# Two cached-attention problems on one core: wo loaded last in runs of up to 16 KB, with every head placed by selector matmuls

## The chip, the cores and the metric

The kernel runs on one core of one Trainium2 chip. The metric is the time of one execution on the device, in microseconds. A program on one core has only this one core's span to report. The profile's span starts at the first instruction and is about 1.7 us shorter than the timed execution (831.1 against 832.8 us in the profiled run of the kernel before).

## The reference

Two independent attention problems, A and B, with one query token each, 32 heads of 128 dimensions, and their results side by side:

```python
q      = (x @ wq) -> 32 heads x 128                 # x: 512, wq: 512 x 4096
k, v   = cache[:, Sk-W:, :]                         # A: W = 16384 keys, B: W = 4096 keys
p      = softmax(q . k / sqrt(128))
o      = p . v                                      # 32 x 128
out    = o.reshape(4096) @ wo                       # wo: 4096 x 512 (4 MB in bf16)
result = concat(out_A, out_B)                       # 1024 numbers
```

A head of A needs 4 MB of keys and 4 MB of values, and so do four heads of B together. With wq and wo of both problems the core must read 352 MB. The arithmetic on them is small.

## The kernel before

The work comes in units of 4 MB of keys: one head of A, or four heads of B. Each group of four heads of A is followed by one unit of B. A unit has two chunks of 64 keys per partition. For each chunk VectorE multiplies keys by the query (`prod`) and adds the halves (`half`), PE sums the rest into PSUM (`red`) with identity matmuls, VectorE and ACT make the exponentials, and PE multiplies them with the values into `acc` (PV). Loads all go through one queue, issued by SP in program order as buffers come free:

```python
def _load_kv(nc, cx, unit, which, k=0, w=2 * U):
    ...
    for g, h in enumerate(unit.heads):
        src = view[h].rearrange("(p l) d -> p l d", p=P // n)       # 32 KB in a row per partition
        cx.o(nc.sync.dma_start(out=t[g:P:n, k : k + w, :], in_=src[:, k : k + w, :]))
```

After four heads a group ends: PE folds `acc` to 4 rows of 128 (`f_ps`), ACT divides by the sums (`orow`), and 16 tiny matmuls turn the 4 rows into a column form, 128 partitions by 4, whose row order fits a piece of wo with 4 KB in a row per partition:

```python
def _fin_col(nc, cx, gr):
    gr.oc_ps = cx.pst_pool.tile([P, G], F32, tag="ocp", name="oc_ps")
    orow_j = gr.orow[:, :].rearrange("o (a j) -> o j a", j=G)
    for j in range(G):
        for g in range(G):
            cx.o(nc.tensor.matmul(
                gr.oc_ps[32 * g : 32 * g + 32, j : j + 1],
                lhsT=orow_j[:, j, :], rhs=cx.ident[0:G, g : g + 1], start=True, stop=True,
            ))
```

So wo is loaded in pieces of 1 MB between the units' keys and values (`[g p (j f)]`, 4 KB runs), each group adds its 4 output matmuls, and only the last group must be quick. That last group has a path of its own: the last head of A comes last of all, its V is loaded in pieces of 64, 32, 16 and 16 keys, the last 512 KB of wo (in 1 KB runs) stand ahead of the last two pieces, and the last 32 keys' values are used as matmul weights, so that their result is a column at once:

```python
    load_v(u, 0, U)
    load_v(u, U, U - LATE)
    load_wo(stA, last_wo, 1)
    load_v(u, 2 * U - LATE, LATE // 2)
    load_v(u, 2 * U - LATE // 2, LATE // 2)
...
def _late_pv(nc, cx, ch, gr):
    for k in range(U - LATE, U):
        cx.o(nc.tensor.matmul(
            gr.f_ps[:, 0, :], lhsT=u.vt[:, ch.k0 + k, :], rhs=ch.p[:, k // 4, :, k % 4],
            start=False, stop=(k == U - 1), skip_group_check=True,
        ))
def _late_out(nc, cx, gr):
    ... # multiply by 1/sum on VectorE, 8 output matmuls, 2 copies, output DMA
```

The softmax here doesn't subtract the row's maximum and nothing guards it: scores larger than these inputs give would overflow.

## Time and profile before

| | kernel before |
|---|---|
| timed, median (3 runs) | 832.32 us |
| span of the profile | 831.1 us |
| read from HBM | 352.32 MB |
| busy: DMA engines / VectorE / PE / ACT | nearly all of the span / 70% / 50% / 8% |
| last packet of V ends (packet records of the trace) | 826.1 us |

From the page of the kernel before: the span, the share of each engine, the DMA rows of the 40 slices (busy tenths of the 16 DMA engines, and GB/s), and the DMA queues. Queue q1 carries the kernel's loads, q8 instructions that are fetched through the same engines.

```profile
span 831.1 us, 6096 instructions
PE 416.9 (50%) x2512; PEld 142.0 (17%) x2512; DVE 585.1 (70%) x299; ACT 68.6 (8%) x301; POOL 2.9 (0%) x16
...
DMA  9999999999999999999999999999999999999996
GB/s 379 429 436 428 423 442 431 431 428 431 431 430 428 429 429 428 429 432 434 428 431 432 431 427 429 427 432 433 429 430 432 433 431 427 431 429 428 427 427 256
DMA packets 16047, 352.71 MB, mean 424 GB/s; under 512 B 2578, under 2 KB 3092, under 8 KB 5268
...
q1 hardware_dynamic: 15732, 352.33, 99.1%
q8 instruction: 19, 0.31, 0.2%
```

The DMA engines are busy in every slice but the last, at about 430 GB/s. No other engine comes near. So there is almost no gap in the stream of loads, and with the bytes fixed only the time per byte, the first microseconds and the last ones are left to work on.

The table of stretches shows the end. Its columns are the stretch, its length, busy time (and instructions) of PE, PEld, DVE, ACT and POOL, the granted PE clock, the DMA share and GB/s.

```profile
700.00:780.00 80.00, 40.33 (x252) 13.61 (x251) 57.40 (x28) 7.32 (x33) 0.00 (x0) 0.70 1.00 429
...
820.00:821.00 1.00, 1.00 (x24) 0.29 (x12) 0.00 (x0) 0.00 (x0) 0.00 (x0) 1.00 0.98 369
821.00:822.00 1.00, 1.00 (x12) 0.48 (x8) 0.00 (x0) 0.59 (x1) 0.00 (x0) 1.00 0.75 265
823.00:824.00 1.00, 1.00 (x19) 0.47 (x10) 0.15 (x1) 0.36 (x1) 0.00 (x0) 1.00 0.56 211
825.00:826.00 1.00, 1.00 (x7) 0.43 (x5) 0.00 (x0) 0.79 (x2) 0.00 (x0) 1.00 0.15 61
```

The 16 DMA engines do not finish together: the share falls from about 1 at 821 us to nothing at 826 us. PE is busy for the whole of every microsecond from 816 to 827 us.

The last values' packets ended at 826.1 us, and from the end of a load's last packet to an instruction that waits for it about 0.5 us passes.

### The profile page before, as it was taken

How to read it: one execution, taken by the hardware profiler on the slowest of the kernel's cores; microseconds unless marked ns; L12 is line 12 of the kernel's file. 1: busy time of each engine (PE TensorE's matmuls, PEld its weight loads, DVE VectorE, ACT ScalarE, POOL GpSimd, SP SyncE). 2: the span in 40 equal slices, each digit the busy share in tenths (PEclk: the TensorE clock that was granted, in tenths of full speed). 3: DMA queues.
4: the chain of work that ended last, by engine and by line, in shares of the span. 5: the costliest groups of instructions: out<-in, count | busy, mean ns of one | idle time of the engine just before them, and what ended most of it. 6: DMA issues, size and time to landing. Idle time of an engine off the chain costs nothing.

```text
span 831.1 us, 6096 instructions
## 1 busy us (share of the span) xinstructions
PE 416.9 (50%) x2512; PEld 142.0 (17%) x2512; DVE 585.1 (70%) x299; ACT 68.6 (8%) x301; POOL 2.9 (0%) x16
## 2 busy tenths in 40 slices
PE   3357444544454445544455543555554534555356
PEld 1112111211121111211112111121111211121113
DVE  1893667777777766777777776677667776677793
ACT  2100001000110001100010000100001000110011
POOL 1000000000000000000000000000000000000000
PEclk9768657776777656777678657686667767667658
DMA  9999999999999999999999999999999999999996
GB/s 379 429 436 428 423 442 431 431 428 431 431 430 428 429 429 428 429 432 434 428 431 432 431 427 429 427 432 433 429 430 432 433 431 427 431 429 428 427 427 256
DMA packets 16047, 352.71 MB, mean 424 GB/s; under 512 B 2578, under 2 KB 3092, under 8 KB 5268
## 3 DMA queue, kind: packets, MB, share of 16 engines
q1 hardware_dynamic: 15732, 352.33, 99.1%
q8 instruction: 19, 0.31, 0.2%
q14 instruction: 8, 0.07, 0.0%
q10 hardware_dynamic: 288, 0.00, 0.0%
HBM read 352.32 MB, written 0.00 MB: 424 GB/s over the span
## 4 chain that ended last, share of the span: by engine, by line
DMA 65%; DVE 22%; issue 10%; PE 2%; SPq 1%; DVEq 0%; ACTq 0%
DMA kt<-in_A_k_cache_dram 53%; DVE prod L177 13%; DMA kt<-in_B_k_cache_dram 9%; DVE half L189 7%; DMA xTB<-in_B_x_dram 3%; DVE sc L219 2%; SPq L170 1%; PE acc L248 0%; PE red L202 0%; DVE xbB L96 0%; PE late_ps L278 0%; PE outB L386 0%; PE late_ps L290 0%; PE f_ps L345 0%; PE out L324 0%
## 5 line engine op out<-in xcount | busy, mean ns | idle before, releaser
L202 PE MATMUL red<-half,ident 128*128 128x512 bf16 x640 | 258.1, 576 | 380.3 <-DVE half L189 380.3
L177 DVE TENSOR_TENSOR prod<-kt,qallA 128x8192 bf16<-128x8192 bf16 x64 | 283.2, 4426 | 160.1 <-DMA kt<-in_A_k_cache_dram 159.3
L189 DVE TENSOR_TENSOR half<-prod 128x4096 bf16<-128x4096 bf16 x80 | 182.5, 2281 | 0.0
L202 PEld LDWEIGHTS <-ident 128*128 128x128 bf16 x640 | 82.6, 129 | 530.0 <-issue 505.4
L177 DVE TENSOR_TENSOR prod<-kt,qallB 128x8192 bf16<-128x8192 bf16 x16 | 70.8, 4426 | 50.8 <-DMA kt<-in_B_k_cache_dram 50.5
L248 PE MATMUL acc<-vt,pA 128*16 128x512 bf16 x1016 | 88.0, 478 | 11.9 <-DMA vt<-in_A_v_cache_dram 11.9
L226 ACT ACTIVATE pA<-sc 128x64 bf16<-128x64 f32 x64 | 16.4, 256 | 518.2 <-DVE sc L219 518.2
L219 DVE TENSOR_REDUCE sc<-red 128x64 f32<-128x512 f32 x80 | 54.7, 684 | 3.7 <-PE red L202 3.7
L248 PEld LDWEIGHTS <-pA 128*16 128x16 bf16 x1016 | 23.3, 99 | 81.3 <-issue 74.7
L226 ACT ACTIVATE p_sb<-sc,off 128x64 bf16<-128x64 f32 x64 | 21.5, 336 | 104.4 <-DVE sc L219 104.4
L248 PE MATMUL acc<-vt,p_sb 128*16 128x512 bf16 x256 | 23.6, 512 | 0.0
L345 PE MATMUL f_ps<-acc_sb,sel 128*4 128x128 f32 x120 | 15.5, 272 | 4.7 <-ACT acc_sb L259 4.7
L259 ACT COPY acc_sb<-acc 128x512 f32<-128x512 f32 x16 | 9.4, 586 | 83.0 <-PE acc L248 83.0
L124 PE MATMUL q_ps<-wq_t,xbA 128*128 128x512 bf16 x32 | 9.1, 455 | 13.7 <-DVE xbA L96 13.7
L226 ACT ACTIVATION_READ_ACCUMULATOR p_sb<-sc,off 128x1 f32 x64 | 11.9, 186 | 0.0
L226 ACT ACTIVATION_READ_ACCUMULATOR pA<-sc 128x1 f32 x64 | 11.9, 186 | 0.0
L345 PEld LDWEIGHTS f_ps<-acc_sb,sel 128*4 128x4 f32 x120 | 9.3, 86 | 7.4 <-ACT acc_sb L259 5.4
L248 PEld LDWEIGHTS <-p_sb 128*16 128x16 bf16 x256 | 5.9, 104 | 18.7 <-issue 16.9
L386 PE MATMUL outB<-wo_t,oc 128*1 128x512 bf16 x32 | 8.8, 401 | 0.0
L96 DVE COPY xbA<-xTA 128x128 bf16<-128x128 bf16 x4 | 0.6, 221 | 11.4 <-DMA xTA<-in_A_x_dram 11.4
L124 PE MATMUL q_ps<-wq_t,xbB 128*128 128x512 bf16 x32 | 7.2, 379 | 0.7 <-ACT qallB L131 0.7
L386 PE MATMUL outA<-wo_t,oc 128*1 128x512 bf16 x28 | 7.6, 395 | 0.0
(44 smaller groups left out, 60.4 us busy)
## 6 DMA issues: line engine op xcount, KB each, us to landing
kt<-in_A_k_cache_dram SPq DMA_DIRECT2D x32, 4096.0 KB, 27.4
vt<-in_A_v_cache_dram SPq DMA_DIRECT2D x30, 4096.0 KB, 31.1
kt<-in_B_k_cache_dram SPq DMA_DIRECT2D x32, 1024.0 KB, 23.3
vt<-in_B_v_cache_dram SPq DMA_DIRECT2D x32, 1024.0 KB, 27.7
vt<-in_A_v_cache_dram SPq DMA_DIRECT2D x3, 2048.0 KB, 25.0
wq_t<-in_A_wq_dram SPq DMA_DIRECT2D x1, 4096.0 KB
wq_t<-in_B_wq_dram SPq DMA_DIRECT2D x1, 4096.0 KB, 21.8
wo_t<-in_B_wo_dram SPq DMA_DIRECT2D x4, 1024.0 KB, 28.5
```

Source lines behind the costliest of these rows:

```text
L96: cx.o(nc.vector.tensor_copy(st.xb[:, c, g, :].rearrange("p (i r) -> p r i", r=R)[:, g, :], xT[:, c : c + 1].broadcast_to([P, P // R]),))
L124: cx.o(nc.tensor.matmul(q_ps[:, :], lhsT=st.xb[:, c, g, :], rhs=w[:, g, j * (512 // DH) : (j + 1) * (512 // DH), :], start=(g == 0 and c = ...
L170: cx.o(nc.sync.dma_start(out=t[g:P:n, k : k + w, :], in_=src[:, k : k + w, :]))
L177: cx.o(nc.vector.tensor_tensor(out=ch.prod[:, :, :], in0=u.kt[:, ch.k0 : ch.k0 + U, :], in1=q.rearrange("p (o d) -> p o d", o=1).broadcast ...
L189: cx.o(nc.vector.tensor_tensor(out=ch.half[:, :, :], in0=ch.prod[:, :, 0 : DH // 2], in1=ch.prod[:, :, DH // 2 : DH], op=ALU.add,))
L202: cx.o(nc.tensor.matmul(ch.red[:, :, :], lhsT=cx.ident[:, :], rhs=ch.half[:, :, b * W : (b + 1) * W], start=(b == 0), stop=(b == nb - 1),))
L219: cx.o(nc.vector.tensor_reduce(out=sc[:, :], in_=ch.red[:, :, :], axis=AX.X, op=ALU.add))
L226: cx.o(nc.scalar.activation(out=ch.p[:, :, g, :], in_=sc[:, :].rearrange("p (t e) -> p t e", e=4), func=ACT.Exp, scale=SCALE, bias=0.0 if ...
L248: cx.o(nc.tensor.matmul(gr.acc[r : r + 4 * G, :], lhsT=ch.p[:, t, :, :], rhs=u.vt[:, k : k + 4, :], start=(first and t < 4), stop=(ends an ...
L259: cx.o(nc.scalar.copy(gr.acc_sb[:, :], gr.acc[:, :]))
L345: cx.o(nc.tensor.matmul(gr.f_ps[:, 0:DH], lhsT=cx.sel[:, e, :], rhs=gr.acc_sb[:, e * DH : (e + 1) * DH], start=False, stop=(e == 3), skip_ ...
L386: cx.o(nc.tensor.matmul(st.out_ps[0:1, :], lhsT=gr.oc[:, j : j + 1], rhs=st.wo_t[i][:, g, j * st.DN : (j + 1) * st.DN], start=(gr.i == 0 a ...
```

## The change

The intent is to read wo in long runs and to have nothing but a few output matmuls behind the last byte. All of wo is loaded after the last V, into key buffers that are free by then (32 KB per partition, the size of wo). A partition holds 32 rows of wo in a row: two pieces of 16 KB for A, then 16, 8, 4, 2 and 2 KB for B, so that little is left to do behind the last landing. For that, element `[p, j]` of the attention result must be number 32 p + j of all 4096. A group's 4 rows are put in place by 4 selector matmuls that add into one PSUM tile for all groups; the column form goes, and so does the special path of the last group, with its cut V, and the swap of the last two units.

```diff
+def _load_wo(nc, cx, st, j0, n):
+    J = st.wo.shape[0] // P
+    if j0 == 0:
+        st.wo_t = cx.kt_pool.tile([P, J, st.DN], BF16, tag="kt", name=f"wo{st.name}")
+    src = st.wo.rearrange("(p j) f -> p j f", j=J)
+    cx.o(nc.sync.dma_start(out=st.wo_t[:, j0 : j0 + n, :], in_=src[:, j0 : j0 + n, :]))
...
 def _fin_col(nc, cx, gr):
-    ... 16 matmuls of 4 x 32 by 4 x 1
+    st = gr.st
+    J = st.wo.shape[0] // P
+    R = DH // J
+    at = (len(st.groups) - 1 - gr.i) * G * R
+    for r in range(R):
+        cx.o(nc.tensor.matmul(
+            cx.oc_ps[:, st.oc_at : st.oc_at + J],
+            lhsT=cx.place[0:G, r, at : at + P],
+            rhs=gr.orow[:, r * J : (r + 1) * J],
+            start=(cx.oc_first and r == 0), stop=(gr.i == len(st.groups) - 1 and r == R - 1),
+            skip_group_check=True,
+        ))
+    cx.oc_first = False
...
-def _late_sums / _late_fold / _late_pv / _late_sum_before / _late_out / _fin_cast / _fin_out
+def _out(nc, cx, st, j0, n):        # 2 matmuls of 256 columns for each of n rows of wo
+    ...
...
-    units[-2:] = units[:-3:-1]
...
-    load_v(u, 0, U)
-    load_v(u, U, U - LATE)
-    load_wo(stA, last_wo, 1)
-    load_v(u, 2 * U - LATE, LATE // 2)
-    load_v(u, 2 * U - LATE // 2, LATE // 2)
+    pieces = [(stA, 0, J // 2), (stA, J // 2, J // 2)]
+    j0 = 0
+    for x in (J // 2, J // 4, J // 8, J // 16, J // 16):
+        pieces.append((stB, j0, x))
+        j0 += x
+    for p in pieces:
+        ld.add(None if p[1] else "kt", lambda p=p: _load_wo(nc, cx, *p))
...
-    ... the end of the last group
+    for ch in waiting:
+        fin_pe()
+        fin_dve()
+        pv(ch)
+    while fins:
+        fin_pe()
+        fin_dve()
+    for p in pieces:
+        _out(nc, cx, *p)
```

More of the change, by code (lines that the diff above doesn't have):

```diff
@@ L18 @@
 U = 64
-LATE = 32
 SCALE = 1.0 / math.sqrt(DH)
@@ L132, in _q, with _load_kv @@
     cx.loads.release(st.wq_tag)
-def _load_wo(nc, cx, st, i, part=None):
-    if part != 1:
-        st.wo_t[i] = cx.wo_pool.tile([P, 2, G * st.DN], BF16, tag="wo", name="wo_t")
-    t = st.wo_t[i]
-    n = G * DH
-    if part is None:
-        src = st.wo[2 * i * n : 2 * (i + 1) * n, :]
-        cx.o(nc.sync.dma_start(
-            out=t[:, :, :], in_=src.rearrange("(g p j) f -> p g (j f)", g=2, j=G)
-        ))
-        return
-    src = st.wo[(2 * i + part) * n : (2 * i + part + 1) * n, :]
-    if part == 0:
-        cx.o(nc.sync.dma_start(out=t[:, 0, :], in_=src.rearrange("(p j) f -> p (j f)", j=G)))
-    else:
-        cx.o(nc.sync.dma_start(
-            out=t[:, 1, :].rearrange("p (h f) -> p h f", h=G),
-            in_=src.rearrange("(h p) f -> p h f", h=G),
-        ))
-def _load_kv(nc, cx, unit, which, k=0, w=2 * U):
+def _load_wo(nc, cx, st, j0, n):
[4 more added lines that the diff above has]
+    cx.o(nc.sync.dma_start(out=st.wo_t[:, j0 : j0 + n, :], in_=src[:, j0 : j0 + n, :]))
+def _load_kv(nc, cx, unit, which):
     pool, tag = (cx.kt_pool, "kt") if which == "k" else (cx.vt_pool, "vt")
-    if k == 0:
-        setattr(unit, tag, pool.tile([P, unit.keys, DH], BF16, tag=tag, name=tag))
-    t = getattr(unit, tag)
+    t = pool.tile([P, unit.keys, DH], BF16, tag=tag, name=tag)
+    setattr(unit, tag, t)
     st = unit.st
@@ L169, in _load_kv @@
         src = view[h].rearrange("(p l) d -> p l d", p=P // n)
-        cx.o(nc.sync.dma_start(out=t[g:P:n, k : k + w, :], in_=src[:, k : k + w, :]))
+        cx.o(nc.sync.dma_start(out=t[g:P:n, :, :], in_=src))
 def _mult(nc, cx, ch):
@@ L233, in _softmax, with _pv @@
         ))
-def _pv(nc, cx, ch, t0=0, t1=U // 4):
+def _pv(nc, cx, ch):
     u, gr = ch.unit, ch.unit.group
     first = u.heads[0] == gr.heads[0] and ch.i == 0
-    ends = u.heads[-1] == gr.heads[-1] and ch.last_of_unit
-    if first and t0 == 0:
+    last = u.heads[-1] == gr.heads[-1] and ch.last_of_unit
+    if first:
         cx.turn = 1 - cx.turn
         gr.acc = cx.acc[cx.turn]
-    for t in range(t0, t1):
+    T = U // 4
+    for t in range(T):
         r = 32 * (t % 4)
@@ L252, in _pv @@
             start=(first and t < 4),
-            stop=(ends and t >= t1 - 4),
+            stop=(last and t >= T - 4),
         ))
@@ L256, in _pv @@
         cx.loads.release("vt")
-    if ends:
+    if last:
         gr.acc_sb = cx.accs_pool.tile([P, 4 * DH], F32, tag="accs", name="acc_sb")
         cx.o(nc.scalar.copy(gr.acc_sb[:, :], gr.acc[:, :]))
-    return gr if ends else None
-def _late_sums(nc, cx, gr):
-    gr.f_ps = cx.psout_pool.tile([P, 2, G], F32, tag=f"out{gr.st.name}", name="late_ps")
-    for i in range(2):
-        cx.o(nc.tensor.matmul(
-            gr.f_ps[:, 1, :], lhsT=cx.ones_f[:, :], rhs=gr.cs[:, i, :],
-            start=(i == 0), stop=(i == 1), skip_group_check=True,
-        ))
-    gr.recip = cx.singles.tile([P, G], F32, tag="late_recip", name="late_recip")
-    cx.o(nc.vector.reciprocal(gr.recip[:, :], gr.f_ps[:, 1, :]))
@@ L275, in _late_fold @@
-def _late_fold(nc, cx, gr):
-    for e in range(4):
-        cx.o(nc.tensor.matmul(
-            gr.f_ps[:, 0, :],
-            lhsT=gr.acc_sb[:, e * DH : (e + 1) * DH],
-            rhs=cx.sel[:, e, :],
-            start=False, stop=False, skip_group_check=True,
-        ))
-def _late_pv(nc, cx, ch, gr):
-    u = ch.unit
-    for k in range(U - LATE, U):
-        cx.o(nc.tensor.matmul(
-            gr.f_ps[:, 0, :],
-            lhsT=u.vt[:, ch.k0 + k, :],
-            rhs=ch.p[:, k // 4, :, k % 4],
-            start=False, stop=(k == U - 1), skip_group_check=True,
-        ))
@@ L298, in _late_sum_before @@
-def _late_sum_before(nc, cx, st):
-    n = st.DN // 2
-    st.out2 = []
-    for t in range(2):
-        o = cx.red_pool.tile([P, n], F32, tag="red", name="out2")
-        st.out2.append(o[32 * t : 32 * t + 1, :])
-        cx.o(nc.tensor.matmul(
-            st.out2[t],
-            lhsT=cx.ones_f[0:1, 0:1],
-            rhs=st.row[0:1, t * n : (t + 1) * n],
-            start=True, stop=False, skip_group_check=True,
-        ))
-def _late_out(nc, cx, gr):
-    st = gr.st
-    n = st.DN // 2
-    gr.oc = cx.ends.tile([P, G], BF16, tag="oc", name="oc")
-    cx.o(nc.vector.tensor_tensor(
-        out=gr.oc[:, :], in0=gr.f_ps[:, 0, :], in1=gr.recip[:, :], op=ALU.mult
-    ))
-    for j in range(G):
-        for t in range(2):
-            f = j * st.DN + t * n
-            cx.o(nc.tensor.matmul(
-                st.out2[t],
-                lhsT=gr.oc[:, j : j + 1],
-                rhs=st.wo_t[gr.i // 2][:, 1, f : f + n],
-                start=False, stop=(j == G - 1), skip_group_check=True,
-            ))
-    row = cx.singles.tile([1, st.DN], BF16, tag="late_row", name="late_row")
-    for t, copy in enumerate((nc.vector.tensor_copy, nc.scalar.copy)):
-        cx.o(copy(row[0:1, t * n : (t + 1) * n], st.out2[t]))
-    cx.o(nc.sync.dma_start(out=cx.out[0, 0:1, st.at : st.at + st.DN], in_=row[:, :]))
@@ L336, in _fin_fold @@
+    return gr if last else None
 def _fin_fold(nc, cx, gr):
@@ L340, in _fin_fold @@
         cx.o(nc.tensor.matmul(
-            gr.f_ps[:, DH : DH + 1], lhsT=gr.cs[:, i, :], rhs=cx.ones_f[:, 0:1],
+            gr.f_ps[:, DH : DH + 1], lhsT=gr.cs[:, i, :], rhs=cx.ones_col[:, 0:1],
             start=(i == 0), stop=(i == 1), skip_group_check=True,
@@ L353, in _fin_row @@
 def _fin_row(nc, cx, gr):
-    recip = cx.ends.tile([G, 1], F32, tag="recip", name="recip")
+    recip = cx.small.tile([G, 1], F32, tag="recip", name="recip")
     cx.o(nc.vector.reciprocal(recip[:, :], gr.f_ps[:, DH : DH + 1]))
-    gr.orow = cx.ends.tile([G, DH], BF16, tag="orow", name="orow")
+    gr.orow = cx.small.tile([G, DH], BF16, tag="orow", name="orow")
     cx.o(nc.scalar.activation(
@@ L362, in _fin_col @@
 def _fin_col(nc, cx, gr):
-    gr.oc_ps = cx.pst_pool.tile([P, G], F32, tag="ocp", name="oc_ps")
-    orow_j = gr.orow[:, :].rearrange("o (a j) -> o j a", j=G)
-    for j in range(G):
-        for g in range(G):
-            cx.o(nc.tensor.matmul(
-                gr.oc_ps[32 * g : 32 * g + 32, j : j + 1],
-                lhsT=orow_j[:, j, :],
-                rhs=cx.ident[0:G, g : g + 1],
-                start=True,
-                stop=True,
-            ))
-def _fin_cast(nc, cx, gr):
-    gr.oc = cx.ends.tile([P, G], BF16, tag="oc", name="oc")
-    cx.o(nc.vector.tensor_copy(gr.oc[:, :], gr.oc_ps[:, :]))
@@ L381, in _fin_out @@
-def _fin_out(nc, cx, gr):
-    st = gr.st
-    i, g = gr.i // 2, gr.i % 2
-    last = gr.i == st.in_row - 1
-    for j in range(G):
-        cx.o(nc.tensor.matmul(
-            st.out_ps[0:1, :],
-            lhsT=gr.oc[:, j : j + 1],
-            rhs=st.wo_t[i][:, g, j * st.DN : (j + 1) * st.DN],
-            start=(gr.i == 0 and j == 0),
-            stop=(last and j == G - 1),
-        ))
-    if g == 1:
-        cx.loads.release("wo")
-    if last:
-        done = st.in_row == st.H // G
-        st.row = cx.singles.tile(
-            [1, st.DN], BF16 if done else F32, tag=f"row{st.name}", name=f"row{st.name}"
-        )
-        cx.o(nc.scalar.copy(st.row[0:1, :], st.out_ps[0:1, :]))
-        if done:
-            cx.o(nc.sync.dma_start(
-                out=cx.out[0, 0:1, st.at : st.at + st.DN], in_=st.row[0:1, :]
-            ))
+    st = gr.st
@@ new lines, in _fin_col @@
+    J = st.wo.shape[0] // P
[11 more added lines that the diff above has]
+def _out(nc, cx, st, j0, n):
+    J = st.wo.shape[0] // P
+    if j0 == 0:
+        st.oc = cx.singles.tile([P, J], BF16, tag=f"oc{st.name}", name=f"oc{st.name}")
+        cx.o(nc.vector.tensor_copy(st.oc[:, :], cx.oc_ps[:, st.oc_at : st.oc_at + J]))
+    w = st.DN // 2
+    out = [o[r : r + 1, :] for o, r in zip(cx.out_ps, st.out_rows)]
+    for j in range(j0, j0 + n):
+        for x in range(2):
+            cx.o(nc.tensor.matmul(
+                out[x],
+                lhsT=st.oc[:, j : j + 1],
+                rhs=st.wo_t[:, j, x * w : (x + 1) * w],
+                start=(j == 0),
+                stop=(j == J - 1),
+            ))
+    if j0 + n == J:
+        row = cx.singles.tile([1, st.DN], BF16, tag=f"row{st.name}", name=f"row{st.name}")
+        cx.o(nc.vector.tensor_copy(row[0:1, 0:w], out[0]))
+        cx.o(nc.scalar.copy(row[0:1, w:], out[1]))
+        cx.o(nc.sync.dma_start(out=cx.out[0, 0:1, st.at : st.at + st.DN], in_=row[0:1, :]))
@@ L433 @@
     cx.singles = pool("singles", 1)
-    cx.small = pool("small", 2)
-    cx.ends = pool("ends", 2)
+    cx.small = pool("small", 4)
     cx.kt_pool = pool("kt", 2)
@@ L439 @@
     cx.half_pool = pool("half", 2)
-    cx.wo_pool = pool("wo", 2)
     cx.accs_pool = pool("accs", 2)
@@ L448 @@
     ld = cx.loads = _Loads()
-    ld.free = {"kt": 2, "vt": 2, "wo": 2}
-    cx.one = cx.singles.tile([1, 1], BF16, tag="one", name="one")
-    nc.gpsimd.memset(cx.one[:, :], 1.0)
-    cx.ones_f = cx.singles.tile([P, P], F32, tag="ones_f", name="ones_f")
-    nc.gpsimd.memset(cx.ones_f[:, :], 1.0)
+    ld.free = {"kt": 2, "vt": 2}
+    cx.ones_col = cx.singles.tile([P, 1], F32, tag="ones_col", name="ones_col")
+    nc.gpsimd.memset(cx.ones_col[:, :], 1.0)
     ones_mat = cx.singles.tile([P, P], BF16, tag="ones_mat", name="ones_mat")
@@ L487 @@
     )
+    J = A_wo.shape[0] // P
+    R = DH // J
+    w = 2 * P - G * R
+    ones_row = cx.singles.tile([G, R * w], BF16, tag="ones_row", name="ones_row")
+    nc.gpsimd.memset(ones_row[:, :], 1.0)
+    cx.place = cx.singles.tile([G, R, w], BF16, tag="place", name="place")
+    nc.gpsimd.affine_select(
+        out=cx.place[:, :, :],
+        in_=ones_row[:, :].rearrange("p (r c) -> p r c", r=R),
+        pattern=[[-1, R], [1, w]],
+        compare_op=ALU.is_equal,
+        fill=0.0,
+        base=-(P - G * R),
+        channel_multiplier=-R,
+    )
     cx.pA = []
@@ L499 @@
         nc.vector.memset(cx.acc[i][:, :], 0.0)
+    cx.oc_ps = cx.pst_pool.tile([P, 512], F32, tag="ocp", name="oc_ps")
+    cx.oc_first = True
+    cx.out_ps = [
+        cx.psout_pool.tile([P, A_wo.shape[1] // 2], F32, tag=f"out{i}", name=f"out{i}")
+        for i in range(2)
+    ]
     def problem(name, x, k_cache, v_cache, wq, wo, sk0, W, at):
@@ L507, in problem @@
         st.v_view = v_cache[0, :, sk0 : sk0 + W, :]
-        st.out_ps = cx.psout_pool.tile([1, st.DN], F32, tag=f"out{name}", name=f"out{name}")
-        st.wo_t = {}
+        st.oc_at, st.out_rows = (0, (0, 32)) if name == "A" else (64, (64, 96))
         st.mix = 1 if W == SkA else G
-        st.in_row = st.H // G - (W == SkA)
         st.groups = [_Group(st, i) for i in range(st.H // G)]
@@ L532 @@
         chunks += u.chunks
-    def load_k(u):
-        ld.add("kt", lambda: _load_kv(nc, cx, u, "k"))
-    def load_v(u, k=0, w=2 * U):
-        ld.add(None if k else "vt", lambda: _load_kv(nc, cx, u, "v", k, w))
-    def load_wo(st, b, part=None):
-        ld.add(None if part else "wo", lambda: _load_wo(nc, cx, st, b, part))
+    ld.add("vt", lambda: _load_wq(nc, cx, stA, "vt"))
     n = len(units)
-    per = 2 * G
-    last_wo = stA.H // per - 1
-    ld.add("vt", lambda: _load_wq(nc, cx, stA, "vt"))
-    for i, u in enumerate(units):
+    for i in range(n + 1):
         if i == G - 1:
             ld.add("kt", lambda: _load_wq(nc, cx, stB, "kt"))
-        load_k(u)
-        if u.heads[0] % per == (3 if u.st is stA else 0):
-            b = u.heads[0] // per
-            load_wo(u.st, b, 0 if u.st is stA and b == last_wo else None)
-        if i == n - 2:
-            load_v(units[i - 1], 0, U)
-        elif i == n - 1:
-            load_v(units[i - 2], U, U)
-            load_v(units[i - 1])
-        elif i:
-            load_v(units[i - 1])
-    load_v(u, 0, U)
-    load_v(u, U, U - LATE)
-    load_wo(stA, last_wo, 1)
-    load_v(u, 2 * U - LATE, LATE // 2)
-    load_v(u, 2 * U - LATE // 2, LATE // 2)
+        if i < n:
+            ld.add("kt", lambda u=units[i]: _load_kv(nc, cx, u, "k"))
+        if i:
+            ld.add("vt", lambda u=units[i - 1]: _load_kv(nc, cx, u, "v"))
+    pieces = [(stA, 0, J // 2), (stA, J // 2, J // 2)]
[5 more added lines that the diff above has]
+        ld.add(None if p[1] else "kt", lambda p=p: _load_wo(nc, cx, *p))
     _load_x(nc, cx, stA)
@@ L582, in fin_pe @@
                 _fin_col(nc, cx, gr)
-                gr.stage = 3
-            elif gr.stage == 4:
-                _fin_out(nc, cx, gr)
                 gr.stage = 9
@@ L593, in fin_dve @@
                 gr.stage = 2
-            elif gr.stage == 3:
-                _fin_cast(nc, cx, gr)
-                gr.stage = 4
     def pv(ch):
@@ L616 @@
         _red(nc, cx, ch)
-        if len(waiting) > 1 and c < len(chunks) - 2:
+        if len(waiting) > 1:
             pv(waiting.pop(0))
         prev = ch
-    end = prev.unit.group
     _softmax(nc, cx, prev)
-    while waiting[0].unit is not prev.unit:
-        pv(waiting.pop(0))
-    _late_sum_before(nc, cx, end.st)
-    _late_sums(nc, cx, end)
-    fin_pe()
-    fin_dve()
-    pv(waiting.pop(0))
-    fin_pe()
-    fin_dve()
-    _pv(nc, cx, prev, 0, (U - LATE) // 4)
-    fin_pe()
-    _late_fold(nc, cx, end)
-    _late_pv(nc, cx, prev, end)
-    _late_out(nc, cx, end)
+    waiting.append(prev)
+    for ch in waiting:
[7 more added lines that the diff above has]
+        _out(nc, cx, *p)
 _INS = ['A_x', 'A_k_cache', 'A_v_cache', 'A_wq', 'A_wo', 'B_x', 'B_k_cache', 'B_v_cache', 'B_wq', 'B_wo']
```

## The prediction

> **What bounds the kernel.** DMA. The page gives 352.33 MB read in a span of 831.1 us; the table of stretches gives 427 to 433 GB/s with a DMA share of 1.00 from 20 to 780 us. The Trainium skill ("DMA: Bandwidth & Descriptors", section "Where 436 GB/s comes from") states a fabric ceiling of 435 GB/s; this trace's 431 agrees. VectorE (70% busy), PE (50%) and ACT (8%) have slack: VectorE idles 210 us in front of its products, waiting for keys. So only bytes (unchanged), time per byte, and the ends, where not all 16 engines are busy, can move the time. The head (loads start at 1.8 us) stays. In the tail, by the DMA packet records, the first engine runs dry at 821.0 us, the last data packet ends at 826.1 us, and the kernel ends 5.0 us later.
>
> **What the change does, costed with packet durations of this trace** (32 KB 1220 ns, 16 KB 616, 8 KB 315, 4 KB 163, 1 KB 48.7; 2 KB an estimate between them, 86 ns; 16 engines).
> - wo: now 1920 packets of 4 KB and 512 of 1 KB, 21.1 us. After: 384 of 16 KB, 128 of 8 KB, 128 of 4 KB, 256 of 2 KB, 20.0 us. Saved 1.2 us.
> - The last three V loads are no longer cut to 16, 8 and 4 KB runs: 19.9 us becomes 19.5. Saved 0.4 us.
> - Both are on the DMA path: the last data packet should end 1.5 us earlier, near 824.6 us.
> - Tail after the last packet. Now 0.5 us to the matmuls, 32 column matmuls with V as weights (0.95 us), multiply (0.16), 8 output matmuls (0.60), copies (0.41), output DMA to the end (2.2); PE is busy from 815 us on with earlier groups. After: 0.5 us, 4 output matmuls (0.4), copies (0.45), output DMA 2.2. About 1.4 us shorter. The output DMA stays; the skill (same page, "Anatomy of one DMA") puts about 2.0 us fixed cost on a DMA, and the 2.2 us agrees.
> - Moved off the path: softmax, fold, selector matmuls and PV of the last unit finish under 20 us of wo loads. Removed: 240 tiny column matmuls (4.4 us of PE) and 60 output matmuls; added: 64 selector matmuls, 128 output matmuls of 256 columns. PE has slack.
>
> **Sum:** 831.1 - 1.5 - 1.4 = 828.2 us span; timed, 832.3 becomes about **829.4 us**, 80% range 826.8 to 831.8. Chances: faster by over 2% 0.01; within 2% 0.975; slower by over 2% 0.015.
>
> **What would show it.** DMA share still 1.00 in the middle; 4 KB packets down from 2176 to 128; last data packet near 824.6 us; the chain ending in a wo landing, a few output matmuls, two copies and a DMA, with no PV, fold or VectorE product in its last 8 us; 3.6 us from last packet to end. The 5 us spread of the engines' finishing times should remain: it is between engines, not from this tail.
>
> **What would make it wrong.** (1) A hole in the queue: the last V load waits for a PV two units back and has no K load ahead of it as cover; I work out about 10 us less slack than in the middle (20 us from issue to landing, not 31). If engines run dry, several us are lost. (2) wo B waits for VectorE's last product; slack about 13 us. (3) 128 output matmuls at the halved clock (0.50 in several stretches) could end after the last landing: +2 us. (4) The spread can shift by 1 to 2 us.

## More of the kernel before

The chain of waits that ended last, in order of time (start, length, what):

```profile
777.84 22.65 DMA kt<-in_A_k_cache_dram
...
800.58 3.58 DVE prod L177
...
815.12 3.57 PE red L202 x8
...
825.76 0.99 PE late_ps L278 x8
826.75 0.82 PE late_ps L290 x32
...
827.80 0.65 PE out L324 x8
828.45 0.40 DVE late_row L332
```

This chain does not end in a DMA wait. It goes from the landing of the last keys (800.5 us) through VectorE and then without a gap through PE, up to the matmuls with the last values (L290).

## The result, and the profile after

| | before | after |
|---|---|---|
| timed, median of 4 runs each | 832.55 us (832.24 to 833.14) | 829.79 us (829.14 to 830.35) |
| ratio | | 0.9966 (95% interval 0.9948 to 0.9983) |
| timed again, 5 runs (the first experiment) | 832.49 us | 829.16 us, ratio 0.9959 |
| span of the profile | 831.1 us | 827.4 us |
| last packet of loaded data ends | 826.1 us | 823.9 us |
| from there to the end of the span | 5.0 us | 3.5 us |

Ratios are the mean time of one kernel's runs over that of the other's of the same rounds, so they are not quite the ratio of the medians quoted here. The change is real, 0.3 to 0.4%. The four runs of the kernel after fall into two pairs, 829.14 and 829.28 us, and 830.30 and 830.35 us; what separates the pairs is not on record. The profile after is that of the fastest run (829.14 us), the profile before that of a run at 832.8 us, a little above its median. So the spans differ by 3.7 us where the medians differ by 2.8 and 3.3 us.

The page of the kernel after, the same lines as before:

```profile
span 827.4 us, 5769 instructions
PE 403.7 (49%) x2368; PEld 138.7 (17%) x2368; DVE 584.7 (71%) x286; ACT 68.1 (8%) x301; POOL 4.5 (1%) x17
...
DMA packets 13902, 352.69 MB, mean 426 GB/s; under 512 B 2482, under 2 KB 2484, under 8 KB 2868
...
q1 hardware_dynamic: 13588, 352.33, 99.2%
q8 instruction: 18, 0.29, 0.1%
```

The bytes are the same. Packets of 2 to 8 KB are fewer, and none of 1 KB are left but the two output rows.

```profile
700.00:780.00 80.00, 39.89 (x229) 13.54 (x229) 59.21 (x27) 6.38 (x30) 0.00 (x0) 0.70 1.00 431
...
820.00:821.00 1.00, 1.00 (x22) 0.80 (x19) 0.00 (x0) 0.00 (x0) 0.00 (x0) 1.00 0.68 272
821.00:822.00 1.00, 0.44 (x10) 0.22 (x6) 0.00 (x0) 0.00 (x0) 0.00 (x0) 1.00 0.55 211
823.00:824.00 1.00, 0.85 (x12) 0.51 (x12) 0.00 (x0) 0.00 (x0) 0.00 (x0) 1.00 0.12 43
824.00:825.00 1.00, 0.52 (x8) 0.09 (x3) 0.18 (x1) 0.15 (x1) 0.00 (x0) 1.00 0.00 0
```

The decline of the DMA share has the same shape, about 2 us earlier, and PE now has gaps in it. The chain of waits, from where it joins the last V:

```profile
783.16 18.98 DMA vt<-in_B_v_cache_dram
802.14 0.02 issue
802.16 22.20 DMA woB<-in_B_wo_dram
824.36 0.04 issue
824.40 0.43 PE out L303 x4
824.83 0.41 DVE rowB L312
```

This chain does end in a DMA: the last piece of wo, then 4 output matmuls, one copy, and the output DMA.

### The profile page after: what moved, and what is told of

The parts are those of the page before. It is cut to its first block, busy times and chain, and to the rows that moved or that the text cites. A ratio compares the mean times of both kernels' runs of the same rounds, so it can differ in the third digit from the quotient of the medians.

```text
span 827.4 us, 5769 instructions
## 1 busy us (share of the span) xinstructions
PE 403.7 (49%) x2368; PEld 138.7 (17%) x2368; DVE 584.7 (71%) x286; ACT 68.1 (8%) x301; POOL 4.5 (1%) x17
## 4 chain that ended last, share of the span: by engine, by line
DMA 68%; DVE 20%; issue 9%; PE 1%; SPq 1%; ACT 0%; DVEq 0%
DMA kt<-in_A_k_cache_dram 49%; DVE prod L161 12%; DMA kt<-in_B_k_cache_dram 12%; DVE half L173 6%; DMA wq_t<-in_B_wq_dram 3%; DMA woB<-in_B_wo_dram 3%; DMA vt<-in_B_v_cache_dram 2%; DVE sc L203 2%; SPq L154 1%; PE q_ps L123 1%; PE red L186 0%; PE acc L233 0%; ACT qallB L130 0%; DVEq L161 0%; DVE recip L267 0%
## 5 line engine op out<-in xcount | busy, mean ns | idle before, releaser
L186 PE MATMUL red<-half,ident 128*128 128x512 bf16 x640 | 253.3, 567 | 388.1 <-DVE half L173 374.4
L233 PE MATMUL acc<-vt,p_sb 128*16 128x512 bf16 x256 | 20.5, 450 | 0.2 <-DMA vt<-in_B_v_cache_dram 0.2
L269 ACT ACTIVATE orow<-f_ps,recip 4x128 bf16<-4x128 f32 x16 | 5.7, 358 | 20.5 <-DVE recip L267 20.5
L267 DVE RECIPROCAL recip<-f_ps 4x1 f32<-4x1 f32 x16 | 2.4, 150 | 6.0 <-PE f_ps L257 6.0
```

What stands on the lines that cost most here:

```text
L186: cx.o(nc.tensor.matmul(ch.red[:, :, :], lhsT=cx.ident[:, :], rhs=ch.half[:, :, b * W : (b + 1) * W], start=(b == 0), stop=(b == nb - 1),))
L233: cx.o(nc.tensor.matmul(gr.acc[r : r + 4 * G, :], lhsT=ch.p[:, t, :, :], rhs=u.vt[:, k : k + 4, :], start=(first and t < 4), stop=(last an ...
L267: cx.o(nc.vector.reciprocal(recip[:, :], gr.f_ps[:, DH : DH + 1]))
L269: cx.o(nc.scalar.activation(out=gr.orow[:, :], in_=gr.f_ps[:, 0:DH], func=ACT.Copy, scale=recip[:, 0:1]))
```

## The experiments

The theory (called the queue theory in the expectations): the time is the end of the DMA stream plus a serial tail behind the last packet. The stream got shorter by packet overheads, and the tail by the work moved away. Rivals: the gain is PE work taken off the end; or it is having wo out of the middle of the stream, whatever its runs; or run lengths explain all of it. All runs below had 5 rounds.

### The changed kernel again

No edit. Expected:

> The changed kernel, unedited, as the yardstick on this chip. Queue theory (time is the end of the DMA stream plus a serial tail of 3.5 us): 829.2 to 830.4 us, ratio to before 0.9966 within 0.001. Every rival expects the same.

Measured: 829.16 us (829.03 to 829.25) against 832.49 us, ratio 0.9959 (0.9947 to 0.9972). In its profile the last packet ends at 823.8 us and the span is 827.3 us. This is the yardstick for the other runs: 3.3 us gained. The expected ratio is met, and the time lies at the lower edge of the expected range.

### wo in 1 KB runs, and in 4 KB runs

The rows (or blocks of four rows) of one piece go to every second place in the tile, so that neighbours in memory are no longer neighbours in the buffer and the runs are cut. DMAs, their order, their waits and the matmuls stay. In the short form:

```diff
+def pos(j):                       # 1 KB; for 4 KB: (j % 16 // 4 * 2 + j // 16) * 4 + j % 4
+    return j % 16 * 2 + j // 16
...
+    r = min(1, n)                 # 4 KB: min(4, n)
+    b = pos(j0)
-    cx.o(nc.sync.dma_start(out=st.wo_t[:, j0 : j0 + n, :], in_=src[:, j0 : j0 + n, :]))
+    cx.o(nc.sync.dma_start(
+        out=st.wo_t[:, :, :].rearrange("p (j r) f -> p j (r f)", r=r)[:, b // r : b // r + 2 * (n // r) - 1 : 2, :],
+        in_=src[:, j0 : j0 + n, :].rearrange("p (j r) f -> p j (r f)", r=r),
+    ))
...
-                rhs=st.wo_t[:, j, x * w : (x + 1) * w],
+                rhs=st.wo_t[:, pos(j), x * w : (x + 1) * w],
```

> Only the run length of the wo loads is changed: the rows of a piece go to every second row place, so that all 8 MB go as 8192 packets of 1 KB; same DMAs, same order, same matmuls, right result. Queue theory: 8192 x 48.7 ns / 16 engines = 24.9 us against 20.0 us, so 4.9 us slower than the changed kernel, near 834.5 us, and slower than before. Rival (the gain is from PE work taken off the end, run length does not matter): no change, within 0.5 us. Rival (the gain is from taking wo out of the middle of the stream, whatever its runs): no change.

> As before this one, but with the 4 KB runs that the kernel before had (1920 packets of 4 KB, 256 of 2 KB). Queue theory: 0.7 us slower than the changed kernel, near 830.4 us, so over half of the gain over before stays. If the whole gain was the run length, it falls back to 832.5 us; if run length is nothing, 829.7 us.

Measured: 1 KB runs 833.24 us (833.05 to 833.43), 4.1 us slower than the yardstick and as slow as the kernel before (ratio to it 1.0008, 0.9996 to 1.0021). 4 KB runs 829.83 us (829.80 to 830.75), 0.7 us slower, ratio to before 0.9970. By the packet records the last data packet ends at 827.8 us with 1 KB runs and at 824.7 us with 4 KB runs, against 823.8 us.

So run length counts. For 4 KB the 0.7 us of the expectation is a slip: the packets that it lists (1920 x 163 ns and 256 x 86 ns over 16 engines, 20.9 us, against 20.0 us) make 0.9 to 1.0 us. Measured were 0.7 us by the medians, 0.9 us by the ratios and 0.9 us at the last packet, so the sum of packet times still gives the size. (All five runs, 829.80 us and up, lie above all five of the yardstick, 829.25 us and down.) For 1 KB, 4.9 us were expected and 4.1 us came, and the kernel came out level with the kernel before, where the expectation had it slower. The trace shows that the sum counts too much here. The 1 KB packets took 50.8 ns in the mean, so by their sum the stream would be 6.0 us longer, but their recorded times overlap: the DMA share is 1.08 from 804 to 820 us, where it is 1.00 in the changed kernel from 804 to 812 us. The last packet came 4.0 us later. The rivals in which run length is nothing fall. So does the one that it is everything: with the 4 KB runs of before, 2.7 of 3.3 us stay.

### The last V after wo

```diff
-        if i:
+        if i and i < n:
             ld.add("vt", lambda u=units[i - 1]: _load_kv(nc, cx, u, "v"))
...
         ld.add(None if p[1] else "kt", lambda p=p: _load_wo(nc, cx, *p))
+    ld.add("vt", lambda: _load_kv(nc, cx, units[-1], "v"))
...
     waiting.append(prev)
+    fin_pe(); fin_dve(); fin_pe()
+    for p in pieces[:2]:
+        _out(nc, cx, *p)
...
-    for p in pieces:
+    for p in pieces[2:]:
```

> The changed kernel with the last V loaded after wo; output A is computed ahead of the last PV, output B after it; right result. Same bytes and packets, so the last data packet should end at the same time (824 us in the profile). Queue theory: after it come 0.5 us, 32 PV matmuls, copy, fold, row, selector and cast (5.1 us by the changed kernel's trace), 64 output matmuls (3.3), copies and output DMA (2.7): 11.6 us instead of 3.5, so about 8 us slower, near 838 us. Rival (position is nothing, the gain is the bytes' efficiency): no change.

Measured: 840.71 us (839.09 to 842.80), 11.5 us slower than the yardstick. The last packet ends at 824.3 us, so the stream is as good as unchanged (0.5 us later), and the loss is all behind it. From the timeline of this run (start, length, engine, line, what):

```profile
824.85 3.59 PE L233 MATMUL acc<-vt,p_sb 128*16 128x512 bf16 x32 [16.75 <-DMA vt<-in_B_v_cache_dram]
...
832.24 6.19 PE L303 MATMUL out<-woB,ocB 128*1 128x256 bf16 x64 [0.28 <-DVE ocB L298]
```

The direction is the queue theory's, and the rival that position is nothing falls. The size was 3.5 us short. The profile, which is that of the slowest of the five runs (842.80 us), shows the reason in the granted clock: it was 0.50 to 0.54 in these stretches, and the 64 output matmuls took 6.2 us, where A's 64 took 3.7 us at full clock earlier in the same run (from 804.4 us). From PV to the cast 7.4 us passed instead of the 5.1 us that were expected. These two terms are 5.2 us more than expected, all of what the profile's tail (16.7 us instead of 11.6) had too much. So an estimate of tail work that is taken from stages at full clock was too short here. The half clock began at 810.2 us, while PE sat idle; what sets the clock was not tested.

### No taper

```diff
-    for x in (J // 2, J // 4, J // 8, J // 16, J // 16):
+    for x in (J // 2, J // 2):
```

> The changed kernel with B's wo in two pieces of 2 MB instead of 16, 8, 4, 2 and 2 rows. Queue theory: 320 fewer small packets save 0.15 us of DMA, but 32 output matmuls (1.9 us) instead of 4 (0.4) stand after the last landing: 1.3 us slower than the changed kernel, near 831 us. Rival (the end is set by PE or by the output DMA only): no change.

Measured: 832.00 us (830.64 to 832.24), 2.8 us slower than the yardstick, which was timed on another chip, so compare it as the ratio to before too: 0.9989 (0.9976 to 1.0001), against 0.9959, which makes 2.5 us. Its last packet ends at 823.7 us, as in the yardstick (823.8 us). From its timeline:

```profile
824.27 2.68 PE L303 MATMUL out<-woB,ocB 128*1 128x256 bf16 x32 [2.96 <-DMA woB<-in_B_wo_dram]
```

The 32 matmuls start 0.5 us after the last packet and run partly at the lower clock (0.62 from 825 to 826 us, 0.50 after), so they took 2.68 us where 1.9 us had been counted. That is one reason why more than the expected 1.3 us was lost. So the taper is needed; without it about three quarters of the gain is gone.

### What ends the kernel before

Three kernels take something away from the kernel before. Their outputs are wrong, which doesn't matter for the times. The first takes 512 KB of wo out of the stream ahead of the last two V pieces. The second takes the end of B's last group off PE. The third does both.

```diff
 # less wo
-    load_wo(stA, last_wo, 1)
...
-                rhs=st.wo_t[gr.i // 2][:, 1, f : f + n],
+                rhs=st.wo_t[gr.i // 2][:, 0, f : f + n],
 # less PE
-        st.in_row = st.H // G - (W == SkA)
+        st.in_row = st.H // G - 1
-        done = st.in_row == st.H // G
+        done = st.name == "B"
-        if gr is not None:
+        if gr is not None and gr.i < gr.st.in_row:
```

> The kernel before without its last 512 KB of wo (512 packets of 1 KB, 1.56 us of 16 engines), which stands in the queue ahead of the last two V pieces; the last group of A uses other rows of wo, so the result of A is wrong on purpose. If the DMA stream alone set the end of the kernel before, it gets 1.5 us faster (831.0). If its PE chain (busy from 815 to 828 us) was just as late, it gets 0.0 to 0.4 us faster, and the change needed to take PE work off the end too for its gain. I expect the latter: the trace shows PE arriving at the last V's matmuls at 826.5 us and the data at 826.1 plus 0.5.

> The kernel before without the end of B's last group (its fold, 16 column matmuls and 4 output matmuls, some 2 us of PE inside the last 12 us); B lacks that group, so the result is wrong on purpose. All loads stay. If PE alone set the end, 2 us faster. Two limits at the same place (PE arriving at 826.5, the last V at 826.1 plus 0.5 us): 0 to 0.3 us faster, like the run that only shortened the DMA stream (0.0).

> Both cuts together: without the last 512 KB of wo and without the end of B's last group. Two limits at the same place: now 1.3 to 1.6 us faster (last V at 824.6 plus 0.5 us, PE there before it), though each cut alone gives nothing. If some third thing sets the end (the products on VectorE, the output DMA), still 0.

Measured, as ratios to the kernel before of the same rounds:

| | time | ratio (95% interval) | last V packet ends | start of the last matmuls on V (L290) | span |
|---|---|---|---|---|---|
| before | 832.3 to 832.5 us | 1 | 826.1 us | 826.6 us | 831.1 us |
| less wo | 832.75 us | 1.0000 (0.9987 to 1.0012) | 824.6 us | 826.6 us | 831.0 us |
| less PE | 832.43 us | 1.0001 (0.9988 to 1.0014) | 825.7 us | second half 826.2 us | 830.7 us |
| less of both | 831.37 us | 0.9988 (0.9974 to 1.0001) | 824.4 us | 825.4 us | 829.8 us |

Less wo: the data came 1.5 us earlier, and nothing happened, since PE got there no earlier. This is its chain of waits:

```profile
825.75 0.98 PE late_ps L278 x8
826.74 0.82 PE late_ps L290 x32
```

Less PE: now PE is early, and the same matmuls wait for the data, in its timeline (the bracket gives the idle time before it and what ended it):

```profile
824.91 0.56 PE L290 MATMUL late_ps<-pA,vt 128*128 128x4 bf16 x16 [0.20 <-DMA vt<-in_A_v_cache_dram]
826.17 0.59 PE L290 MATMUL late_ps<-pA,vt 128*128 128x4 bf16 x16 [0.71 <-DMA vt<-in_A_v_cache_dram]
```

These matmuls end 0.8 us earlier than in the kernel before, but half of that is lost right behind them: the granted clock is 0.50 from 825.7 us on, and the 8 output matmuls took 1.01 us, where they had taken 0.60 us at full clock:

```profile
827.01 1.01 PE L324 MATMUL out<-wo_t,oc 128*1 128x256 bf16 x8 [0.26 <-DVE oc L318]
```

Both cuts together gave 0.9 us (medians 832.27 and 831.37), less than the 1.3 to 1.6 us expected, and with an interval that just touches 1; but its slowest run (831.77 us) is below the fastest of the kernel before in the same rounds (832.07 us) and of less PE (832.11 us). Its span is 1.3 us shorter. Its chain again runs through PE, from `red` on:

```profile
814.91 3.57 PE red L202 x8
...
825.49 0.82 PE late_ps L290 x32
```

So the kernel before ended on two limits at nearly the same place, its stream and its PE chain, and shortening either alone gained nothing that could be seen in the time. The change takes both away at once.

### More instructions, and fewer

The profile shows instruction fetches in packets of 16 KB on the same DMA engines. The finishing times of the engines differ by steps of about that length (0.9 to 1.2 us, against 1.07 us a fetch): in the run without taper, the last load ended (by the 4-byte packets, 16 a load, that report it) at 819.0 to 819.3 (5 of them), 820.2, 821.1, 822.1 to 822.5 (7) and 823.7 us (2). To test whether fetches cost time in a kernel that is bound by DMA, 32 tiny matmuls were put ahead of each chunk's `red`, where PE idles:

```diff
+    for b in range(32):
+        cx.o(nc.tensor.matmul(
+            ch.red[:, 0, :], lhsT=cx.ident[:, :], rhs=cx.ident[:, 0:W],
+            start=True, stop=True, skip_group_check=True,
+        ))
     for b in range(nb):
```

> The changed kernel with 32 more tiny matmuls (8 columns, and a weight load each) ahead of each chunk's 8 reducing matmuls, in time in which PE idles: 5120 instructions more, which is 320 KB, 20 more fetches of 16 KB on the same 16 DMA engines (1.07 us each in the trace). Queue theory with the finishing spread put down to fetches: 20 x 1.07 / 16 = 1.3 us more on average, 1 to 3 us slower in time, 38 fetches in the profile, and the engines that finish last are those with most fetches. Rival (PE instructions are free as long as PE has slack; the spread has another cause): no change, within 0.5 us.

Measured: 832.50 us (832.33 to 832.86), ratio to before 0.9998 against 0.9959 of the unedited changed kernel: 3.3 us lost. PE is 56% busy and has slack. From the page and the table of stretches of this run:

```profile
q8 instruction: 38, 0.62, 0.3%
```

```profile
700.00:780.00 80.00, 46.15 (x483) 19.55 (x481) 58.83 (x27) 6.84 (x32) 0.00 (x0) 0.71 1.00 431
...
820.00:821.00 1.00, 0.47 (x6) 0.00 (x0) 0.50 (x2) 0.36 (x1) 0.00 (x0) 0.50 0.70 289
823.00:824.00 1.00, 0.94 (x10) 0.61 (x11) 0.00 (x0) 0.00 (x0) 0.00 (x0) 0.50 0.50 205
825.00:826.00 1.00, 1.00 (x13) 0.59 (x10) 0.00 (x0) 0.00 (x0) 0.00 (x0) 0.50 0.45 180
```

The first engines run dry when they did in the changed kernel (0.70 against 0.68 at 820 us). But then the share stays near one half up to 826 us, where it had fallen to nothing by 824 us. This fits 20 extra fetches that were not spread over 16 engines but carried by about eight (20 x 1.07 / 8 = 2.7 us each, as an estimate of the average), and the stream ends with the last engine (827.6 us instead of 823.8 us). The fetches' own times fit that too: in all twelve traces, but for a few outliers, they repeat with a period of eight (in the kernel before 1108, 1100, 1087, 1018, 1025, 1074, 1069 and 1060 ns, then 1100, 1107, 1086 and so on). The loads' own packets also took 1.0 us more per engine (821.5 against 820.5 us); whether the fetches or the other work of the extra matmuls did that was not separated. The mean cost, 1.3 us, would have been too small by more than half. The Trainium skill ("Runtime: NRT & Kernel Launch", section "Instruction fetch mechanics") says that a sequencer refills in 16 KiB blocks through a DMA queue of its own, and that crossing a block is mostly hidden. The trace agrees on the block (16 KB packets). The page speaks of the sequencer's own wait; what was not hidden here is the cost to the loads. Fetches do not explain the whole spread of the unedited kernel: its 18 take 19 us in all, and the finishing times above lag the first engine's by 36 us in all. The rest stays open.

The other way round, one more halving on VectorE and half the `red` matmuls:

```diff
+    ch.quarter = cx.half_pool.tile([P, U, DH // 4], BF16, tag="quarter", name="quarter")
+    cx.o(nc.vector.tensor_tensor(
+        out=ch.quarter[:, :, :], in0=ch.half[:, :, 0 : DH // 4],
+        in1=ch.half[:, :, DH // 4 : DH // 2], op=ALU.add,
+    ))
...
-    nb = DH // 2 // W
+    nb = DH // 4 // W
...
-            rhs=ch.half[:, :, b * W : (b + 1) * W],
+            rhs=ch.quarter[:, :, b * W : (b + 1) * W],
```

> The changed kernel with one more halving on VectorE (128 x 2048, an estimate of 1.15 us, 80 times; VectorE idles 200 us) and 4 instead of 8 reducing matmuls a chunk: 1280 trace records less on PE, 40 KB of instructions, 2 to 3 fetches of 16 KB fewer. If fetches on the slowest DMA engine set the end: 15 or 16 fetches, and 0 to 1.1 us faster (0 if none of those dropped fell on the engine that ends last). Rival (VectorE comes close to the limit, 82% busy): slower by 1 us or more with DMA share below 1.00 in the middle.

Measured: 829.90 us (829.14 to 830.54), ratio to before 0.9971 (0.9959 to 0.9984). There were 16 fetches instead of 18 (and 640 fewer PE records, not the 1280 of the expectation), VectorE was 82% busy, and the DMA share kept its nines in the middle, so neither theory's number came: no gain, and 0.7 us lost by the medians or 1.0 us by the ratios, whose intervals overlap. The last packet ended at 824.7 us, 0.9 us later than the yardstick's. That two fetches fewer are no use because the engine that ends last still has its share is a guess. Which engine gets which fetch was not found out; the records do not name the engine.

## Why the prediction was right or wrong

The prediction was right: 829.4 us predicted, 829.79 us and 829.16 us measured. That the two are this close is in part luck: one term was too small by 0.7 us, and one step was argued past a second limit (the third point and the last). Point by point:

- **Bound by DMA, middle unchanged.** Right: DMA share 1.00 at 429 and 431 GB/s in the same stretch.
- **Run length of wo, 1.2 us.** Right in kind, and in size where it could be isolated: going back from 16 KB to the 4 KB runs cost 0.7 to 0.9 us, where the packet durations make 0.9 to 1.0 us. The rest of the 1.2 us (the 1 KB part and the cuts of B's taper) was not isolated.
- **Last data packet near 824.6 us, 1.5 us earlier.** It ended at 823.9 and 823.8 us, 2.2 us earlier. The mis-sized term is one that was left out. By the packet records the time of q1's packets per engine fell by 2.7 us (823.2 to 820.5 us), of which 1.6 us are the cuts that the prediction counted. Another 1.1 us come from the 10240 packets of 32 KB that both kernels share: their mean fell from 1220.1 to 1218.4 ns. A third of this lies in the first 30 us. Its cause is open; the mean was 1218.4 to 1218.7 ns in the five versions of the changed kernel with 18 fetches, and 1219.9 ns with 38 fetches; but it was 1219.9 to 1220.2 ns in the four versions of the kernel before, with 19, so the number of fetches does not explain it.
- **Tail 1.4 us shorter.** Right: 5.0 us became 3.5 us, and 3.6 us was predicted. That it rests on the taper and on having no PV behind the last byte is shown by the runs that undo these (2.8 and 11.5 us lost). The output DMA's fixed time stayed, 2.1 us from its issue at 825.30 us to the end of the span. The Trainium skill ("DMA: Bandwidth & Descriptors", "Anatomy of one DMA") fits a fixed cost of about 2.0 us to DMAs that GpSimd issues; this one was issued by SP and took about as long.
- **No hole in the queue, wo B in time.** Right: the last V was issued at 782.0 us, the last pieces of wo by 802.5 us, and the DMA share is 0.99 or above from 784 to 792 us.
- **128 output matmuls might end late at half clock.** Not so with the taper: the last 4 started 0.5 us after the last packet. Output matmuls did run late at a lower clock where they were not spread over the landings (V last, no taper).
- **A gap in the argument.** "Both are on the DMA path" took the kernel before to end with its stream. It ended with two limits at once: 1.5 us off the stream alone gained 0.0 us, some PE work off alone 0.0 us, both about 1 us. The sum came out right because the change also removes the PE chain from the end, which the prediction listed as moved off the path without asking whether the saving on the stream depended on it.

The spread of 5 us between the first and the last DMA engine remained, as predicted: on average an engine sits idle for some 2.7 us of it (the missing DMA shares from 819 to 824 us added up), beside the 3.5 us of tail in which all of them do. Adding fetches made it larger. No version here removed it, and none beat the changed kernel.

## What to carry to other kernels

In a kernel bound by one stream, cost the change in packet times and in what stands behind the last packet, and order the loads so that the last bytes need the least work. Before counting a saving at the end, check that the chain of waits really ends in the stream: here two limits within half a microsecond of each other had to be moved together. And in this kernel, whose DMA engines had no gap, instructions on an engine with slack were not free: 5120 more of them came with 20 more fetches through the DMA engines and cost 3.3 us.

## What the Trainium skill lacked or had wrong

- "Runtime: NRT & Kernel Launch", "Instruction fetch mechanics", calls the cost of crossing a 16 KiB block mostly hidden, which is said of the sequencer. What a block takes from the loads is lacking: in this DMA-bound kernel 20 more blocks (18 to 38 fetches of 1.07 us) came with 3.3 us, 2.5 times their mean over 16 engines, which fits about eight engines carrying them. No page that was read warns of instruction count in this sense.
- "DMA: Bandwidth & Descriptors", "Where 436 GB/s comes from", says without a condition that the HBM side, about 358 GB/s, binds HBM to SBUF transfers; only a note in the section before it ties that figure to both cores of an HBM domain streaming. Here one core read 427 to 433 GB/s from HBM from 20 to 780 us; the fabric figure of 435 in the same section is the one that fits, and the section itself notes that its own 16 MB measurement (425 GB/s) is near it.
- The same page, "Measured", gives time by transfer size for SWDGE, not by run length. The packet records here give it for loads issued by SP: 1220 ns for 32 KB, 616 ns for 16 KB, 163 ns for 4 KB, 48.7 ns for 1 KB (50.8 ns where 8192 of them followed each other). Wo's 8 MB in runs of 4 KB instead of up to 16 KB cost 0.7 to 0.9 us.
- No page that was read says how unequally the 16 engines finish one long stream of loads issued by SP: here within 5 us, in the run without taper in steps of 0.9 to 1.2 us.
